# Weights laid out for the DMA, two streams of FFN weights, and a later output projection, in a two-layer transformer kernel

## Chip, cores, metric

One core of one Trainium2 chip. The time is the device time of one execution in microseconds; a kernel is judged by the median of several executions, and compared with another by runs on the same chip. An execution that is profiled also has its own time: the span on a profile's page is about 1.7 us shorter than that time.

## The reference

Two layers, each of them twice layer norm and a residual: a local attention (32 heads of 32, window of 8 positions at distance 2), then a feed-forward part (FFN) with squared ReLU. The sequence has 2048 rows, the model width is 1024, the FFN width 3584; both layers use the same weights.

```python
x = x + A(layernorm(x), wqkv, wo)          # qkv = x @ wqkv; window softmax; @ wo
x = x + B(layernorm(x), w1, b1, w2, b2)    # relu(x @ w1 + b1)**2 @ w2 + b2
x = x + A(layernorm(x), wqkv, wo)
x = x + B(layernorm(x), w1, b1, w2, b2)
```

## The kernel before

The sequence is cut into blocks of 512 rows: 4 per layer, 8 in all, called block 0 to block 7. The program is first recorded as a list of operations with priorities. A planner then orders them for each engine with assumed durations, so that one block's attention on VectorE runs beside another block's matmuls. The FFN matmuls of blocks 1 to 7 use a seven-product scheme: of the seven products of weight quarters, three use raw quarters of w1 ("raw") and four use sums and differences ("made"), which block 0 computes and stores in DRAM.

Weights pass through 1 MB buffers. At most six of them (`w=6`) are live, and they are given out in the order in which they were created. A load is issued when a buffer comes free.

```python
p.caps.update(..., w=6, ..., wl=2)

def weights(self, ap, kt, wide=False):
    b = Buf("8K", "w", [128, 8, 512], BF)
    if wide:   # qkv and wo
        self.dma(lambda: b[:].rearrange("p (a b) n -> p a (b n)", a=4), lambda: ap, (), [(b, 0)], 1.05, name="w")
    ...

def copy_w1(self, after):            # raw quarters of w1, DRAM to DRAM, 21 copies
    for i, (dp, pr) in enumerate(self.order1):
        if pr in (1, 2, 4):
            ...
            self.dma(lambda i=i: self.w1s[i // 4][:, i % 4], lambda k=k, c0=c0: self.w1_v[:, 4 * k:4 * k + 4, c0:c0 + 256], ...)
```

The FFN's first part reads tiles of four products in order of use. The projections take every eighth column of the loaded weights, so that a head's parts land where the attention wants them:

```python
for j, (d, pr) in enumerate(self.order1):          # SF1, blocks 1 to 7
    if j % 4 == 0:
        ...
        self.dma(lambda w=w, n=n: w[:, 0:n], lambda j=j: self.w1s[j // 4][:], ...)
    steps[d](pr, w, j % 4, *rhs[pr])

nc.tensor.matmul(pq[:], wv[:, kd % 4, c0:D:8], xnT[:, :, kd, :], ...)   # SQ, wv a view of [128, 4, 1024]
```

Near the end, the output projection (SW) of block 7 is recorded before the FFN's second part (SF2) of block 6:

```python
if u == NU - 2:
    self.SW(u + 1)
(self.SF2 if u else self.SF2_plain)(u)
```

The softmax here doesn't subtract the row's maximum and nothing guards it: scores larger than these inputs give would overflow.

## Time and profile before

| | before |
|---|---|
| median of the first 4 runs | 1209.71 us (1208.51 to 1210.4) |
| profiled run | 1210.4 us, span 1208.7 us, granted clock 0.997 |
| PE busy | 1182.8 us, 98% |

The first part of the page of the kernel before (busy us, share of the span, number of instructions):

```profile
PE 1182.8 (98%) x6876; PEld 744.2 (62%) x6923; DVE 977.9 (81%) x1551; ACT 670.5 (55%) x1238; POOL 5.0 (0%) x13
```

A busy PE need not be a fast one, so its pitch (the time from the start of one matmul to the start of the next) must be checked: in the timeline below, 40 projections of 512 columns take 8.63 us from start to start (19.79 to 28.42), 215.8 ns each. This is the pitch of every undisturbed run of such matmuls in the trace. Two groups, kept apart by shape, are the projections and their weight loads (count | busy us, mean ns of one | idle before):

```profile
L596 PE MATMUL pq<-xnA,w 128*128 128x512 f16 x1512 | 331.1, 379 | 0.0
L596 PEld LDWEIGHTS <-w 128*128 128x128 bf16 x1512 | 216.6, 143 | 109.4
```

Each matmul lasts 379 ns by the profile, but the next starts 215.8 ns after it, so matmuls overlap. A weight load with the stride of eight columns takes 143 ns. The other 128-column loads take 98 ns, and both fit under 215.8 ns.

What PE waits for, kernel before (us in total, times, longest):

```profile
PE Y L913 <- DMA w<-in_B_w_dram: 5.4, 2, 3.5
PE pk L989 <- POOL grp L240: 5.3, 1, 5.3
PE pq L601 <- DMA w<-in_A_wqkv_dram: 3.7, 2, 2.5
PE Z L859 <- DVE rr L836: 1.7, 4, 0.4
PE Z L913 <- DMA w<-tw: 1.0, 2, 0.6
PE X L913 <- DMA w<-in_B_w_dram: 0.9, 1, 0.9
```

L601 and L596 are the projections, L859 the FFN's first part, L913 its second part. `in_B_w_dram` is w1 or w2, `tw` the made parts of w2. Where these waits lie is seen in PE's timeline of the kernel before (start us, duration, what, [idle before <- releaser]), first in the head:

```profile
12.37 0.66 PE L601 MATMUL pq<-xnA,w 128*128 128x256 f16 x4 [1.21 <-DMA w<-in_A_wqkv_dram]
15.55 1.07 PE L601 MATMUL pq<-xnA,w 128*128 128x256 f16 x4 [2.52 <-DMA w<-in_A_wqkv_dram]
16.41 1.06 PE L532 MATMUL pt<-ident,xn 128*128 128x128 f16 x8
17.27 2.68 PE L601 MATMUL pq<-xnA,w 128*128 128x256 f16 x16
19.79 8.80 PE L596 MATMUL pq<-xnA,w 128*128 128x512 f16 x40
28.42 1.04 PE L601 MATMUL pq<-xnA,w 128*128 128x256 f16 x8
```

and in block 6, where SF1 hands over to SF2:

```profile
1051.20 0.38 PE L370 MATMUL X<-b2r,pick 128*128 128x512 bf16 x1
1052.52 1.67 PE L913 MATMUL X<-w,r 128*128 128x512 bf16 x6 [0.94 <-DMA w<-in_B_w_dram]
...
1057.50 1.04 PE L859 MATMUL Z<-xnB,w 128*128 128x256 f16 x8
1062.02 4.04 PE L913 MATMUL Y<-w,r 128*128 128x512 bf16 x12 [3.48 <-DMA w<-in_B_w_dram]
```

After the wait of 3.48 us, the start-to-start times in the trace are 0.215 us for six matmuls, then 0.427 us: PE runs at half speed for a while. This text calls such matmuls cold. SyncE's own timeline shows why the loads come late: the two loads of wo go first and hold two buffers.

```profile
1039.16 3.83 SPq L305 DMA_DIRECT2D w<-in_A_wo_dram  x2
1046.15 11.91 SPq L305 DMA_DIRECT2D w<-in_B_w_dram  x4
```

### The profile page before, as it was taken

What the parts mean: (1) busy time and instruction counts of PE and PEld (TensorE: products, weight loads), DVE (VectorE), ACT (ScalarE), POOL (GpSimd) and SP (SyncE); (2) the same over time, 40 slices, a digit from 0 to 9 for tenths busy, and PEclk for the clock granted to TensorE, in tenths of its full rate; (3) what the DMA queues carried; (4) which work ended last, traced back from release to release, by engine and by line L of the source; (5) the groups of instructions that cost most, each with busy time, mean ns of one, the idle gap of its engine ahead of it and who ended that gap; (6) DMA issues with size and microseconds to landing.
All of it is one profiled execution on the core that took longest, in us unless ns stands there. A gap on an engine that the chain in (4) does not pass through costs nothing.

```text
span 1208.7 us, 18037 instructions
## 1 busy us (share of the span) xinstructions
PE 1182.8 (98%) x6876; PEld 744.2 (62%) x6923; DVE 977.9 (81%) x1551; ACT 670.5 (55%) x1238; POOL 5.0 (0%) x13
## 2 busy tenths in 40 slices
PE   6999999999999999999999999999999999989998
PEld 4665544557845687456864578555784557834863
DVE  3799999539999499976999589993999949997562
ACT  5546893189702897049940599317981175624640
POOL 1000000000000000000000000000000000000000
PEclk9999999999999999999999999999999999999999
DMA  9679999968999698978999789997899875689964
GB/s 304 201 212 281 299 338 307 316 210 300 267 366 327 215 334 300 353 262 274 347 303 382 251 267 331 332 337 233 296 333 334 296 235 227 222 290 334 324 226 149
DMA packets 209223, 348.03 MB, mean 288 GB/s; under 512 B 67184, under 2 KB 134000, under 8 KB 196336
## 3 DMA queue, kind: packets, MB, share of 16 engines
q1 hardware_dynamic: 197984, 333.22, 82.2%
q10 hardware_dynamic: 7488, 13.63, 3.1%
q0 software_dynamic: 3664, 0.02, 0.4%
q8 instruction: 54, 0.88, 0.3%
q14 instruction: 33, 0.27, 0.1%
HBM read 292.30 MB, written 46.40 MB: 280 GB/s over the span
## 4 chain that ended last, share of the span: by engine, by line
PE 71%; DVE 11%; ACT 10%; DMA 4%; issue 2%; ACTq 1%; SPq 0%; DVEq 0%
PE X L913 14%; PE pq L596 13%; PE X L859 11%; PE Z L913 7%; PE Z L859 6%; DVE P L640 5%; PE py L743 5%; PE py L361 4%; PE ph L774 4%; DVE P L648 3%; PE Y L913 3%; PE Y L859 3%; ACT xn L453 2%; ACT xn L482 2%; ACT xn L478 2%; DMA w<-in_B_w_dram 2%
## 5 line engine op out<-in xcount | busy, mean ns | idle before, releaser
L596 PE MATMUL pq<-xnA,w 128*128 128x512 f16 x1512 | 331.1, 379 | 0.0
L596 PEld LDWEIGHTS <-w 128*128 128x128 bf16 x1512 | 216.6, 143 | 109.4
L859 PEld LDWEIGHTS <-w 128*128 128x128 f16 (+1 forms) x2544 | 248.8, 98 | 39.1 <-issue 3.3
L640 DVE TENSOR_TENSOR P<-q,k 128x2048 f16<-128x2048 f16 x128 | 152.9, 1222 | 85.1 <-ACT q L609 68.5
L913 PEld LDWEIGHTS <-r 128*128 128x128 f16 x1176 | 115.2, 98 | 144.3 <-issue 9.6
L913 PE MATMUL X<-w,r 128*128 128x512 f16 (+1 forms) x777 | 175.9, 379 | 1.4 <-DMA w<-in_B_w_dram 0.9
L609 ACT CAST k<-pq 128x512 f16<-128x512 f32 x64 | 37.6, 587 | 239.5 <-PE pq L596 238.6
L700 DVE TENSOR_TENSOR pr<-pb,v 128x2048 f16<-128x2048 f16 x128 | 154.3, 1220 | 0.2
L859 PE MATMUL X<-T,w 128*128 128x256 f16 x1104 | 135.4, 273 | 0.6 <-ACT u L833 0.6
L648 DVE TENSOR_TENSOR P<-P,P 128x2048 f16<-128x2048 f16 x96 | 116.1, 1216 | 0.1
L743 PE MATMUL py<-w,o 128*128 128x512 bf16 x496 | 111.5, 379 | 0.8
L847 ACT ACTIVATE r<-rr 128x1024 f16<-128x1024 f16 x98 | 102.5, 1062 | 10.8 <-DVE rr L843 9.5
L833 ACT CAST u<-X 128x512 f16<-128x512 f32 x147 | 84.7, 589 | 38.8 <-PE X L859 35.0
L743 PEld LDWEIGHTS <-o 128*128 128x128 bf16 x512 | 50.0, 98 | 59.6
L703 DVE TENSOR_TENSOR pr<-pr 128x1024 f16<-128x1024 f16 x128 | 85.8, 681 | 0.0
L748 DVE TENSOR_TENSOR xm<-py,xt 128x512 f32<-128x512 f32 x64 | 44.0, 690 | 50.1 <-PE py L743 50.0
L836 DVE TENSOR_TENSOR rr<-u,Z 128x512 f16<-128x512 f16 x98 | 65.4, 681 | 18.9 <-ACT u L833 11.0
L478 ACT ACTIVATE xn<-xm 128x1024 f16<-128x1024 f32 x32 | 33.8, 1056 | 59.9 <-DVE xm L748 57.1
L875 ACT ACTIVATE rr<-X,b1T 128x256 f16<-128x256 f32 x98 | 43.2, 482 | 21.6 <-PE X L859 21.4
L706 DVE TENSOR_TENSOR pr<-pr 128x512 f16<-128x512 f16 x128 | 52.1, 415 | 0.1
L913 PE MATMUL Y<-w,r 128*128 128x512 bf16 x191 | 46.2, 388 | 5.9 <-DMA w<-in_B_w_dram 5.4
L843 DVE TENSOR_SCALAR rr<-rr,b1T 128x256 f16<-128x256 f16 (+1 forms) x196 | 50.8, 312 | 0.3
(108 smaller groups left out, 1328.6 us busy)
## 6 DMA issues: line engine op xcount, KB each, us to landing
w<-w1s SPq DMA_DIRECT2D x78, 1024.0 KB, 7.8
w<-tw SPq DMA_DIRECT2D x56, 896.0 KB, 7.7
w<-in_A_wqkv_dram SPq DMA_DIRECT2D x48, 1024.0 KB, 8.5
w<-in_B_w_dram SPq DMA_DIRECT2D x42, 896.0 KB, 7.3
w<-in_A_wo_dram SPq DMA_DIRECT2D x16, 1024.0 KB, 8.4
xt<-xs SPq DMA_DIRECT2D x32, 512.0 KB, 7.4
w<-in_B_w_dram SPq DMA_DIRECT2D x28, 512.0 KB, 7.0
xs<-xo SPq DMA_DIRECT2D x32, 256.0 KB, 7.1
```

The source lines that it names most:

```text
L478: nc.scalar.activation(out=xn[:], in_=xv(), func=ACTF.Identity, accum_out=s1())
L596: nc.tensor.matmul(pq[:], wv[:, kd % 4, c0:D:8], xnT[:, :, kd, :], start=(kd == 0), stop=(kd == KD - 1))
L640: nc.vector.tensor_tensor(cur[:], q[:, c, None, hb * HB:(hb + 1) * HB].to_broadcast([128, W, HB]), _win_ap(k[:, c, :], HALO + hb * HB, HB) ...
L648: nc.vector.tensor_tensor(other[:], other[:], cur[:], ALU.add)
L700: nc.vector.tensor_tensor(pr[:], pb[:], _win_ap(v[:, c, :], HALO + hb * HB, HB), ALU.mult)
L703: nc.vector.tensor_tensor(pr[:, 0:4, :], pr[:, 0:4, :], pr[:, 4:8, :], ALU.add)
L743: nc.tensor.matmul(py[:], o[:, c, tl * 128:(tl + 1) * 128], wos[c // 4][:].rearrange("p (a b) n -> p a (b n)", a=4)[:, c % 4, db * 512:(db ...
L833: p.add("ACT", act(512), lambda: nc.scalar.copy(us[i][:], X[:]), [(X, 0)], [(us[i], 0)], 1.0, name="u")
L836: p.add("DVE", dve(512, False), lambda: nc.vector.tensor_tensor(r[:, :, m, :], us[i][:], bank[:], ALU.add), [(us[i], 0), (bank, 0)], [(r, ...
L847: p.add("ACT", act(1024), lambda: nc.scalar.activation(out=r2[:, f:f + 2, :].rearrange("p a t -> p (a t)"), in_=r[:].rearrange("p a m t -> ...
L859: nc.tensor.matmul(bank[:, a, :], lw[:, k, a * 128:(a + 1) * 128], rhs(k), start=(start and k == 0 and a == 0), stop=(k == 3), skip_group_ ...
L913: nc.tensor.matmul(banks[q][:], left(jj, q), w[:, j, :], start=(start and jj == 0 and b2 is None), stop=(jj == h - 1), skip_group_check=True)
```

## The change

The intent: let every weight load read long contiguous rows, drop the copies inside DRAM, fetch what PE needs first first, and take wo out of the way of w2. The host rearranges the weights; it does no arithmetic on them. Every matmul stays. In core (cut):

```diff
-        self.w1s = [tc.dram_tile([128, min(4, len(self.order1) - i), 4, 256], F16, ...) for i in range(0, len(self.order1), 4)]
+        self.made1 = [o for o in self.order1 if o[1] not in (1, 2, 4)]
+        self.kept1 = [o for o in self.order1 if o[1] in (1, 2, 4)]
+        self.w1s = [tc.dram_tile([128, min(4, len(self.made1) - i), 4, 256], F16, ...) for i in range(0, len(self.made1), 4)]
...                                                  # copy_w1 and its call are removed
-            x, xv = self.load_x(layer, t, after, tag="x0" if u == 0 else "xt")
+            x, xv = self.load_x(layer, t, after, prio=6.5 if u == 1 else None, tag="x0" if u == 0 else "xt")
...
-            ws[nm] = [self.weights(self.wqkv_v[:, 4 * kh:4 * kh + 4, cols[nm]:cols[nm] + D], 8, wide=True) for kh in range(2)]
+            ws[nm] = [self.weights(self.wqkv["qkv".index(nm), kh], 8) for kh in range(2)]
...
-        for j, (d, pr) in enumerate(self.order1):
+        at, ws = [0, 0], [None, None]
+        for d, pr in self.order1:
+            raw = pr in (1, 2, 4)
+            j, at[raw] = at[raw], at[raw] + 1
             if j % 4 == 0:
...
+                src = self.w1r[j // 4, :, 0:n] if raw else self.w1s[j // 4][:]
...
-            steps[d](pr, w, j % 4, *rhs[pr])
+            steps[d](pr, ws[raw], j % 4, *rhs[pr])
...
         mul("B21", *block(1, 0), Y, True)
+        if between:
+            between()
...
             if u == NU - 2:
-                self.SW(u + 1)
-            (self.SF2 if u else self.SF2_plain)(u)
+                seq, self.seq = self.seq, self.seq + 100
+                def between():
+                    back, self.seq = self.seq, seq
+                    self.SW(u + 1)
+                    self.seq = back
+                self.SF2(u, between)
...
+def _layout(inputs):        # on the host
+    wqkv = a.transpose(3, 0, 2, 5, 1, 6, 4).reshape(3, 2, 128, KD, D // 2)
+    ...                     # w1r: tiles of four raw products; w1, w2: rows of 4 KB and 7 KB
```

So there are five parts: (1) rows of 8 KB for wqkv (2 KB before), 4 KB for w1 (512 B) and 7 KB for w2 (1 KB), with unit-stride weight loads of the projections; (2) no copies of w1 in DRAM; (3) k's weights ahead of block 1's x; (4) two streams of w1 tiles, raw and made, in place of one; (5) SW of block 7 is recorded inside SF2 of block 6, so its buffers come after four w2 loads.

## The prediction

> What bounds the kernel now. The page's first part has PE busy 1182.8 of 1208.7 us (98%) at a granted clock of 0.997, nearly all at its steady rate: in PE's timeline, 40 projections of 512 columns follow each other in 8.63 us, 215.8 ns each. The Trainium skill ("TensorE: Matmul & The Clock Gate", Back-to-back issue gap, warm N/2.4 + 2.5 ns) gives 215.8 ns; the trace agrees, so nothing is left inside these runs. The change keeps every matmul: only the 26 us in which PE is idle can be won, under 2.2%.
>
> Improved without gain. The strided weight loads of the projections take 143 ns against 98 ns for contiguous ones (groups of instructions), but both hide under 215.8 ns. The 21 copies of w1 inside DRAM and its 512 B rows (25,088 packets at 255 GB/s while they run; 8 KB 388) load the DMA at 90 to 210 us, where it is full but PE waits 0.4 us. Both: about 0.
>
> Where PE waits (waits of PE, timeline):
> A. Head. Projections start at 12.37 us, the steady stream at 17.27. The weights of k land at 12.33 and 15.50 because 512 KB of x for the next block go ahead; those of q at 18.78 and 21.80, needed at 23.2. The change puts k first and makes rows 8 KB: k lands at about 9.7 and 12.5 (estimate: 2.75 us per MB, not 3.1), projections start at about 11.3, when the transposed tiles are copied, and q, behind the same bytes as before, at about 19.5 to 21.5 becomes the limit. Gain 3.0 us (1.4 if 8 KB rows are no faster; at most 4.2).
> B. Block 1's last FFN part, 331 to 336 us: 2.4 us behind a w2 load issued when a buffer came free at 329.2, landing 6.9 us later. Row size matters little here (a 1 KB-row load alone landed in 5.15 us, a 7 KB-row one in 5.07), but the new split of w1 loads frees buffers in another order: gain about 1.5.
> C. Waits for tw at 624 and 912: 1.3 us, about 0.5 gained.
> D. Block 6, 1051 to 1067 us: two wo loads (issued 1039 and 1043) take buffers ahead of w2, which lands at 1052.5 and 1062.0; PE loses 1.1 and 3.6 us, then runs cold at 427 ns per matmul: 6.6 us in all. The change takes wo after four w2 loads; wo is not needed before about 1078. Gain 6.3.
> E. DVE waits (five of 0.6 us), launch (first matmul at 5.3 us) and tail (3.5 us) stay. New small stalls, above all in the last block, from the two streams of w1: 1 lost.
>
> Sum: 3.0 + 1.5 + 0.5 + 6.3 - 1 = 10.3 us. Predicted 1199 us, 80% range 1194.5 to 1203.5; faster by over 2% 0.01, same 0.98, slower 0.01.
>
> Right if PE busy stays at 1180 to 1184 us and the span falls by idle time alone; weight loads of projections drop to about 98 ns while their matmuls keep their pitch; the steady stream starts at 13 to 15 us with a short wait for q; no wait for w2 and no cold matmuls at 1050 to 1067.
>
> Wrong if matmuls after contiguous weight loads get a shorter pitch; wo comes late and stalls the last attention; the two streams of w1 run out of buffers in every block; or VectorE, over 97% busy from 60 to 210 us, eats the earlier start.

## The result

| | runs | median us | range |
|---|---|---|---|
| before | 16 | 1208.42 | 1203.61 to 1212.49 |
| changed | 11 | 1201.79 | 1200.25 to 1203.42 |

The ratio is 0.9945 with a 95% interval of 0.9931 to 0.9959: 6.6 us less. A ratio is the mean time of one kernel's runs over that of the other's of the same rounds, so it is not quite the ratio of the medians.

The page of the changed kernel, first part:

```profile
PE 1179.9 (98%) x6876; PEld 673.2 (56%) x6923; DVE 979.1 (81%) x1551; ACT 669.7 (56%) x1238; POOL 5.0 (0%) x13
```

Its two groups of the projections:

```profile
L567 PE MATMUL pq<-xnA,w 128*128 128x512 f16 x1512 | 331.2, 379 | 1.4 <-DMA w<-in_A_wqkv_dram 1.4
L567 PEld LDWEIGHTS <-w 128*128 128x128 bf16 x1512 | 147.8, 98 | 178.5 <-DMA w<-in_A_wqkv_dram 2.1
```

The weight loads fell from 143 to 98 ns each and PE's busy time in these matmuls did not move (331.1 and 331.2 us). What PE waits for now:

```profile
PE pk L964 <- POOL grp L240: 5.3, 1, 5.3
PE Z L886 <- DMA w<-tw: 3.3, 2, 1.9
PE Z L832 <- DVE rr L810: 1.6, 4, 0.4
PE pq L567 <- DMA w<-in_A_wqkv_dram: 1.4, 1, 1.4
PE X L886 <- DMA w<-in_B_w_dram: 1.2, 1, 1.2
```

The 5.4 us of the kernel before for w2 are gone; the wait for tw has grown from 1.0 to 3.3 us. PE's timeline of the changed kernel in the head and in block 6:

```profile
11.66 0.60 PE L571 MATMUL pq<-xnA,w 128*128 128x256 f16 x4 [0.42 <-ACT sm L486]
12.80 0.61 PE L571 MATMUL pq<-xnA,w 128*128 128x256 f16 x4 [0.55 <-DMA w<-in_A_wqkv_dram]
...
15.45 2.75 PE L567 MATMUL pq<-xnA,w 128*128 128x512 f16 x12
19.63 6.22 PE L567 MATMUL pq<-xnA,w 128*128 128x512 f16 x28 [1.43 <-DMA w<-in_A_wqkv_dram]
25.68 1.04 PE L571 MATMUL pq<-xnA,w 128*128 128x256 f16 x8
```

```profile
1049.88 0.38 PE L362 MATMUL X<-b2r,pick 128*128 128x512 bf16 x1
1050.09 1.67 PE L886 MATMUL X<-w,r 128*128 128x512 bf16 x6
...
1055.08 1.04 PE L832 MATMUL Z<-xnB,w 128*128 128x256 f16 x8
1055.95 6.21 PE L886 MATMUL Y<-w,r 128*128 128x512 bf16 x27
```

The same eight matmuls (L601, now L571) start at 25.68 instead of 28.42 us: the head is 2.74 us shorter. In block 6 the waits and the cold matmuls are gone.

The clock in the head is a second difference. In the table of windows (start:end, length, busy us and counts of PE, PEld, DVE, ACT and POOL, then the granted clock, DMA share, GB/s), the kernel before shows PE at half clock for 3.4 us after its wait of 2.52 us:

```profile
15.40:18.80 3.40, 3.25 (x20) 2.77 (x21) 0.69 (x1) 1.50 (x2) 0.00 (x0) 0.50 1.21 346
```

The changed kernel was granted 1.00 there. With the stretch in block 6 (1063.3 to 1066.7 us), the kernel before ran 6.8 us at half clock, which costs about 3.4 us (an estimate: half of 6.8), almost half of what the change won between these two profiles. Its timed runs fit: 42 of them, in the experiments below, were granted 0.996 to 0.999, those at 0.996 took 1210.1 us in the mean and those at 0.999 1206.1 us; the changed kernel's were granted 0.999 to 1.000.

Where the rest went needs a finer count. I took, from each trace, the start-to-start times of consecutive matmuls, subtracted the pitch (215.8 ns for 512 columns, in proportion for fewer), added up what was left over 0.05 us, and left out gaps of one unrecorded matmul (0.19 to 0.235 us without a releaser, outside the head and block 6). This "PE loss" starts at the first matmul, 5.3 us. In the row of block 6 about 0.6 us of either figure is such gaps.

| PE loss, us, from:to us | before | changed | difference | predicted |
|---|---|---|---|---|
| head, 0:60 | 7.7 | 5.0 | -2.7 | -3.0 (A) |
| 60:300 | 1.3 | 1.6 | +0.3 | 0 |
| block 1's SF2, 300:345 | 2.4 | 0.0 | -2.4 | -1.5 (B) |
| blocks 1 to 6, 345:1030 | 4.4 | 8.2 | +3.8 | -0.5 (C) |
| block 6, SF1 to SF2, 1030:1080 | 7.1 | 0.6 | -6.5 | -6.3 (D) |
| block 7, 1080:end | 0.0 | 0.5 | +0.5 | +1 (E, anywhere) |
| sum | 22.9 | 15.9 | -7.0 | -10.3 |

The sum agrees with the spans of the two pages (1208.7 and 1201.7). Between 60 and 300 us, where the copies were taken out, the loss did not fall, although the DMA share at 90 to 120 us fell from 1.00 to 0.48 in the table of windows.

The loss of 3.8 us in the middle is three waits: for the first tw load of block 3 at 620 us (1.6 us; 0.5 before), for w2 in block 4 at 755 us (1.3; none before), and for the first tw load of block 5 at 911 us (2.1; 0.8 before).

### The profile page after: what moved, and what is told of

Same layout as the page of the kernel before. It is cut to its first block, busy times and chain, and to the rows that moved or that the text cites. A ratio compares the mean times of both kernels' runs of the same rounds, so it can differ in the third digit from the quotient of the medians.

```text
span 1201.7 us, 18027 instructions
## 1 busy us (share of the span) xinstructions
PE 1179.9 (98%) x6876; PEld 673.2 (56%) x6923; DVE 979.1 (81%) x1551; ACT 669.7 (56%) x1238; POOL 5.0 (0%) x13
## 4 chain that ended last, share of the span: by engine, by line
PE 67%; DVE 14%; ACT 12%; DMA 3%; issue 2%; ACTq 1%; SPq 0%; DVEq 0%
PE X L886 14%; PE pq L567 12%; PE X L832 11%; PE Z L886 7%; DVE P L610 6%; PE Z L832 6%; PE py L353 4%; DVE P L618 4%; PE Y L886 3%; PE py L713 3%; ACT xn L423 3%; ACT xn L452 3%; PE ph L744 3%; PE Y L832 3%; ACT xn L448 3%
## 5 line engine op out<-in xcount | busy, mean ns | idle before, releaser
L567 PE MATMUL pq<-xnA,w 128*128 128x512 f16 x1512 | 331.2, 379 | 1.4 <-DMA w<-in_A_wqkv_dram 1.4
L832 PEld LDWEIGHTS <-w 128*128 128x128 f16 (+1 forms) x2648 | 259.0, 98 | 41.6 <-issue 3.6
L567 PEld LDWEIGHTS <-w 128*128 128x128 bf16 x1512 | 147.8, 98 | 178.5 <-DMA w<-in_A_wqkv_dram 2.1
L832 PE MATMUL X<-T,w 128*128 128x256 f16 x1160 | 142.3, 273 | 0.8 <-ACT u L807 0.8
L832 PE MATMUL Z<-xnB,w 128*128 128x256 f16 x392 | 49.3, 272 | 1.6 <-DVE rr L810 1.6
```

Of the source, the lines that this page charges most:

```text
L567: nc.tensor.matmul(pq[:], wv(w, c0, kd), xnT[:, :, kd, :], start=(kd == 0), stop=(kd == KD - 1))
L832: nc.tensor.matmul(bank[:, a, :], w[:, wi, k, a * 128:(a + 1) * 128], rhs(k), start=(start and k == 0 and a == 0), stop=(k == 3), skip_gro ...
```

## The experiments

Theories at the start. A: the wo loads held two buffers ahead of w2 in block 6; moving SW gives that part. B: two w1 streams keep two part-used tiles alive, so buffers come free later, the w2 loads are issued later and the tw load after them comes late; this takes 3 to 4 us back. H: in the head the order of loads brings the start forward, and 8 KB rows bring q forward. Rivals: R1, the 7 KB rows of w2 ended the waits of block 6; R2, the 7 KB rows of w2, not the streams, cause the new waits.

### 1. Only the place of SW (`sw_only`, `sw_only_again`)

The kernel before with this alone:

```diff
+        if between:
+            between()            # after B21 in SF2
-            if u == NU - 2:
-                self.SW(u + 1)   # and SF2(u, between) as in the change
```

> The kernel before, with only the place of the last output projection changed (its two wo loads after the first four w2 loads of block 6). Theory A (the wo loads held two buffers ahead of w2): the two waits for w2 at 1051 to 1062 us and the cold matmuls after them go, the rest of the trace stays; minus 6.4 us, ratio 0.9947. Rival R1 (the 7 KB rows of w2, which this kernel does not have, ended those waits): a wait of over 2 us for w2 stays in block 6, ratio 0.998 to 1.000.

Measured: 1203.95 us against 1208.0, ratio 0.9973 (0.9952 to 0.9993). Two of six runs lay at 1208 and 1208.8, so it was run again:

> The kernel before with only the place of the last output projection changed, once more, because two of its six runs lay 4 us above the others and its interval is wide. Theory A: 6.8 us gone in block 6, about 2 us of new waits for w1 in the last block, so ratio 0.9960 to 0.9970 as the four low runs and the new waits say; 0.9947 if the new waits were chance.

Measured: 1203.91 us against 1208.0, ratio 0.9973 (0.9951 to 0.9996), again with one run at 1209. In both profiles the waits for w2 in block 6 and the cold matmuls are gone, without long rows of w2. In exchange block 7 waits for w1 (1.6 and 1.1 us). From PE's waits in `sw_only`:

```profile
PE Y L859 <- DMA w<-w1s: 1.5, 1, 1.5
```

So A holds as a mechanism and R1 falls, but the time won is 3.3 us by the ratio or 4.1 us by the medians, not the 6.4 us that I expected. Part of the difference is the new wait. The other part can be the sample: the two profiled runs of the kernel before took 1210.4 and 1211.3 us, near the slow end of its 1203.6 to 1212.5 us. The clock tells the rest: the three high runs of the twelve were granted 0.995 or 0.996, the nine low ones 0.998 to 1.000. So the high runs had more cold matmuls; none of them was profiled, so where is not known.

### 2. Everything but the place of SW (`sw_back`)

```diff
             if u == NU - 2:
-                self.SF2(u, between)
+                self.SW(u + 1)
+            (self.SF2 if u else self.SF2_plain)(u)
```

> The changed kernel with the last output projection put back before block 6's second FFN part; all layouts and both w1 streams stay. Theory A: PE waits for w2 again at about 1045 to 1060 us, some 6 us with the cold matmuls; ratio 0.999 to 1.001. Rival R1 (row size): no such wait, ratio as the whole change, 0.9945.

Measured: 1205.44 us against 1208.0, ratio 0.9974 (0.9954 to 0.9993). PE waits for w2 in block 6 again, in spite of the 7 KB rows:

```profile
PE Z L886 <- DMA w<-tw: 3.8, 2, 2.0
PE Y L886 <- DMA w<-in_B_w_dram: 2.1, 1, 2.1
PE X L886 <- DMA w<-in_B_w_dram: 1.4, 1, 1.4
```

The loss in block 6 is 3.8 us here, not some 6: the longer wait was 2.1 us, and no cold matmuls followed (0.216 us from start to start). A wait of this size can do it, though: in block 5 of the same execution, after a wait of 1.98 us for tw, the matmuls came 0.427 us apart for 3.4 us.

```profile
910.12 2.96 PE L886 MATMUL Z<-w,s 128*128 128x512 f16 x7 [1.98 <-DMA w<-tw]
```

The rest of the change is then worth about as much (0.9974) as the place of SW alone (0.9973).

### 3. One stream of w1 in the changed kernel (`one_stream`)

Tiles of four products in order of use as before; the raw part of a tile comes from the arranged input and the made part from DRAM, in two transfers.

```diff
+                raw, made = self.parts1[j // 4]
+                slot = {o: i for i, o in enumerate(raw + made)}
+                self.dma(lambda ...: w[:, 0:nr].bitcast(BF), lambda ...: self.w1r[j // 4, :, 0:nr], ...)
+                self.dma(lambda ...: w[:, nr:nr + nm], lambda ...: self.w1s[j // 4][:], ...)
-            steps[d](pr, ws[raw], j % 4, *rhs[pr])
+            steps[d](pr, w, slot[d, pr], *rhs[pr])
```

> The changed kernel with the w1 tiles of before: four products in order of use to a tile, its raw part loaded from the arranged input, its made part from DRAM scratch, in two transfers to the same buffer; no copies inside DRAM. Theory B (two streams keep two part-used tiles alive, so the buffers of the next w2 loads come free later): the waits at about 620 and 911 us for tw fall from 1.6 and 2.1 us to about 0.5 and 0.8, the 1.3 us for w2 at 755 goes; the wait of 2.4 us in block 1 may come back; ratio 0.9920 without it, 0.9940 with it. Rival R2 (those waits come from the 7 KB rows of w2): they stay, ratio 0.9945.

Measured: 1201.02 us against 1208.0, ratio 0.9939 (0.9923 to 0.9955). The waits went as B says: none at 620 and 755 us, 0.6 us at 908. In PE's waits between 340 and 1030 us of this version, one line is left for tw:

```profile
PE Z L889 <- DMA w<-tw: 0.5, 1, 0.5
```

The loss from 345 to 1030 us is 3.7 us. SyncE's timeline of block 3 shows what differs. In the changed kernel, then with one stream:

```profile
602.20 7.89 SPq L304 DMA_DIRECT2D w<-in_B_w_dram  x4
614.09 5.10 SPq L304 DMA_DIRECT2D w<-tw  x4
```

```profile
597.64 0.33 SPq L303 DMA_DIRECT2D w<-in_B_w_dram  x1
...
603.04 6.27 SPq L303 DMA_DIRECT2D w<-in_B_w_dram  x3
615.05 5.09 SPq L303 DMA_DIRECT2D w<-tw  x4
```

With one stream the first w2 load is issued 17.4 us ahead of the first tw load, with two streams 11.9 us. With two the last w2 load landed at 616.04, 1.95 us after the tw load was issued; with one it landed at 615.40, 0.35 us after. PE needs tw about 4.6 us after its issue in both. But 1.0 us came back in block 1 and 1.6 us in block 7, so little of it could be won, and the time does not show it.

### 4. Short rows of w2 in the changed kernel (`w2_rows1k`)

```diff
-        return self.weights(self.w2[k2, n2, :, half * h:(half + 1) * h, :], h)
+        w2 = self.w2.rearrange("(k j p) (m n) -> k m p j n", k=2, p=128, m=2)
+        return self.weights(w2[k2, n2, :, half * h:(half + 1) * h, :], h)
```

> The changed kernel with w2 in its old layout, so rows of 1 KB instead of 7 KB; the same instructions in the same order otherwise. Theory B: the waits at 620, 755 and 911 us stay within 0.5 us each and block 6 has no wait for w2; ratio 0.9935 to 0.9950. Rival R2: the waits in blocks 3 to 5 shrink by 3 us in all, ratio 0.992. Rival R1: a wait of over 2 us for w2 comes back in block 6, ratio 0.997 or more.

Measured: 1201.38 us against 1208.0, ratio 0.9943 (0.9925 to 0.9961). Here B alone missed: with two streams and short rows the two tw waits are gone too. Between 340 and 1030 us only this is left for the DMA (at 615 and 759 us):

```profile
PE Y L890 <- DMA w<-in_B_w_dram: 1.0, 2, 0.6
```

The loss from 345 to 1030 us is 4.3 us, against 8.2 in the changed kernel. No wait for w2 came back in block 6, so R1 falls a second time. For R2 the waits went, but the time did not follow (expected 0.992). Here the first w2 load was issued 12.8 us ahead of the first tw load, little more than the 11.9 us of the changed kernel, so the late issue that B names does not make the wait by itself.

### 5. Both kernels once more (`before_again`, `after_again`)

> The kernel before once more, unchanged, as a control: ratio 1.000 within 0.0015. In its profile the two waits for w2 in block 6 come again; the question is their size. If the cold matmuls after the second wait are a matter of chance, the loss there lies between 3.5 us (without) and 7 us (with them).

> The changed kernel once more, unchanged, for a second profile and a time beside the others of this call. Ratio 0.9945 within 0.0015. Theory B: the waits for tw near 620 and 911 us (1.6 and 2.1 us) are there again, as they were in the version with the last output projection put back; if they are chance, they differ by more than 1 us.

Measured: `before_again` 1208.72 against 1208.41 us, ratio 1.0001 (0.9986 to 1.0015). The loss in block 6 is 8.6 us (about 8.0 without the gaps of unrecorded matmuls), over the 7 us that I expected at most. `after_again` 1200.6 us, ratio 0.9933 (0.9919 to 0.9947). The tw waits are there again (1.9 and 2.2 us), so they are not chance; the w2 wait at 755 us is not, so that one is. One of the two tw waits was put down by the profile to a VectorE operation ("DVE r"); the tw load landed at 620.17 us, 0.04 us before the matmul started, so it was the DMA.

### 6. The head in parts (`k_first`, `x_first`)

`k_first` is the kernel before with the new order of loads; `x_first` the changed kernel with the old order:

```diff
# k_first: + prio=6.5 if u == 1 else None      x_first: - the same
```

> The kernel before, with only the order of the first loads changed: the weights of k ahead of the x of block 1; rows stay 2 KB. Theory H (the order brings the start forward, the rows of 8 KB bring q forward): k lands about 1.6 us earlier than 12.33 and 15.50, q where it did (18.8 and 21.8), so PE starts earlier and then waits for q: gain 0.6 to 1.4 us, ratio 0.9990. Rival (order alone gives the whole 2.7 us): ratio 0.9978 and q lands before 20.5.

> The changed kernel with the x of block 1 again ahead of the weights of k; rows stay 8 KB. Theory H: k lands at about 11.7 and 14.3 us, q at 17 and 19.6 as in the changed kernel; PE gets q just when it has done k; it loses at most 1 us against the changed kernel, ratio 0.9945 to 0.9955. Rival (the order gives the gain): it loses 2 us or more, ratio 0.9962 or more.

Measured: `k_first` 1206.86 us, ratio 0.9989 (0.9977 to 1.0001); `x_first` 1201.09 us, ratio 0.9938 (0.9926 to 0.9950). The start of the same eight matmuls says more:

| | k lands, us | q lands, us | eight matmuls start |
|---|---|---|---|
| before | 12.33, 15.50 | 18.78, 21.80 | 28.42 |
| k_first | 10.79, 13.96 | 18.69, 21.77 | 26.19 |
| x_first | 12.51, 15.08 | 17.66, 20.24 | 28.07 |
| changed | 10.15, 12.76 | 16.98, 19.58 | 25.68 |

In these pairs the order gives 2.2 to 2.4 us, more than the 0.6 to 1.4 of H, and long rows 0.35 to 0.5 us. But the pairs differ in the clock too. `before` and `x_first` ran at half clock for 3.4 us in the head (`x_first` from 16.4 us), about 1.7 us each by the estimate above; `k_first` and the changed kernel did not. `sw_only` has the head of the kernel before and stayed at full clock:

```profile
15.32 0.66 PE L601 MATMUL pq<-xnA,w 128*128 128x256 f16 x4 [2.37 <-DMA w<-in_A_wqkv_dram]
26.65 1.04 PE L601 MATMUL pq<-xnA,w 128*128 128x256 f16 x8
```

So at full clock the order gives 0.46 us (26.65 to 26.19) and the long rows 0.51 us (26.19 to 25.68); the rest of the 2.74 us is the cold stretch. Of five profiles with x first, four went cold in the head; of nine with k first, none. The order seems to keep PE warm by cutting the wait for k's second half from 2.0 to 2.6 us down to 1.5 us or less, but with this few profiles that is likely, not shown. H, which counted waits alone, was near for the order's own share (0.46 us against 0.6 to 1.4) and did not see the clock.

The landings of q show that the rows are faster (1 MB per 2.6 us instead of 3.0 to 3.1), but little of it was won: the planner's order changed as well, `k_first` ran 20 of the 40 projections ahead of the second half of q and waited 0.63 us, the changed kernel ran 12 and waited 1.43 us. My 1.4 us rested on q being needed at 23.2 us. Only its first half is: the second half is needed four matmuls (0.86 us) later. The times of `x_first` and the changed kernel (0.9938 and 0.9933) do not resolve the difference of 2.4 us in the head. Three of the five runs of `x_first` were granted 1.000, which a stretch of 3.4 us at half clock would have brought to 0.999, so most of them had none; that profile of `x_first` also lost only 5.2 us from 345 to 1030 us.

### 7. More of k before q (`after_k5`, `one_k5`)

```diff
-        order = [("k", c0) for c0 in range(3)]
+        order = [("k", c0) for c0 in range(5)]        # and c0 - 5 for q in the loop
```

> The changed kernel with five groups of k instead of three ahead of the first group of q. Theory H (q, behind the same bytes, is what the head waits for): the wait of 1.4 us for q at 19.6 us goes, the head is 1.4 us shorter; waits in blocks 3 to 5 as in the changed kernel; ratio 0.9925 to 0.9935. Rival (VectorE, which then gets its first q later, gives it back by block 1): same time as the changed kernel.

> The same order of k and q with the w1 tiles of before (one stream, each tile loaded in a raw and a made part). No wait for q in the head, waits for tw and w2 in blocks 2 to 5 of at most 1 us in all; about 1 us faster than the changed kernel with this order: ratio 0.9920. If the two streams cost nothing that shows in the time, the two versions are equal within 0.5 us.

Measured: `after_k5` 1200.05 us, ratio 0.9935 (0.9912 to 0.9958); `one_k5` 1198.97 us, ratio 0.9929 (0.9909 to 0.9950), both against 1208.0. The wait for q is gone in both profiles, and the eight matmuls start at 24.45 and 24.29 us. The head's loss is 3.7 us. VectorE does not give it back: the loss from 60 to 300 us is 1.6 and 1.7. The two versions differ by 1.1 us in the medians, within their intervals. The predicted ratio of 0.9920 for `one_k5` was missed, though inside the interval.

### 8. Two streams, short w2 rows, more of k first (`k5_rows1k`)

The edits of 4 and 7 together.

> The changed kernel with five groups of k first and with w2 in rows of 1 KB: a second profile of two w1 streams with short w2 rows. If row size matters beside the streams (the one profile so far had 4.3 us of PE loss between 345 and 1030 us, the profiles with 7 KB rows 5.2 to 8.2), the loss there is again under 5 us and the two waits for tw at 620 and 908 us stay away; if that profile was chance, the loss is 5 us or more and a tw wait of over 1 us is back. Head as in the version with five groups of k first. Ratio 0.9915 to 0.9935.

Measured: 1198.72 us against 1208.55, ratio 0.9917 (0.9903 to 0.9930), the lowest time. The loss from 345 to 1030 us is 3.7 us and the tw waits stay away:

```profile
PE Z L836 <- DVE rr L814: 1.6, 4, 0.4
...
PE Z L890 <- DMA w<-in_B_w_dram: 0.5, 1, 0.5
```

It beats both kernels in the median. Its interval lies wholly below the changed kernel's first one (0.9931 to 0.9959) and overlaps the second (0.9919 to 0.9947), so against the changed kernel it is likely, not proved, to be faster.

### What the profiles of all versions say about tw

Time from issue to landing of the first tw load of SF2:

| w1 streams, w2 rows | version | block 3, us | block 5, us |
|---|---|---|---|
| two, 7 KB | changed | 6.12 | 6.75 |
| | after_again | 6.44 | 6.96 |
| | sw_back | 6.89 | 6.89 |
| | x_first | 4.55 | 6.97 |
| | after_k5 | 6.52 | 4.60 |
| two, 1 KB | w2_rows1k | 5.26 | 4.65 |
| | k5_rows1k | 4.79 | 4.85 |
| one, 7 KB | one_stream | 4.70 | 5.37 |
| | one_k5 | 4.92 | 4.73 |
| one, 1 KB | before | 5.07 | 5.32 |
| | before_again | 4.64 | 4.96 |
| | k_first | 4.73 | 4.56 |
| | sw_only | 4.91 | 4.70 |
| | sw_only_again | 4.74 | 4.58 |

With both new features, 8 of 10 landings take 6.1 to 7.0 us; with one of them or none, 18 of 18 take 4.5 to 5.4 us. PE needs the data about 4.6 us after the issue, so the slow ones cost about 2 us each. Blocks 2 and 4, where PE did not wait for that load, agree: 7 of 10 over 5.7 us with both features, 18 of 18 under 5.5 us without. The two features do it together, and undoing either undoes it. Why long w2 rows still in flight delay the next load, and short ones do not (in `w2_rows1k` w2 was in flight for 3.1 us after the issue, and tw still took 5.26 us), was not tested and stays open.

## Why the prediction was right or wrong

The time fell inside the predicted range (1194.5 to 1203.5) and the class, within 2%, was right. The predicted gain was 10.3 us; it was 6.6 us by the times and 7.0 us by the profiles.

- What bounds it: right. PE's pitch at full clock stayed at 215.8 ns with either weight load, and the span moved with PE's idle and cold time alone. PE busy was to stay at 1180 to 1184 us and is 1179.9.
- Strided weight loads and DRAM copies worth nothing: shown for the loads (143 to 98 ns, busy 331.1 and 331.2 us). For the copies, the loss at 60 to 300 us did not fall with the DMA load there; leaving them out alone was not run. The Trainium skill ("SBUF — State Buffer", Door 1: The DMA port swizzle) says that SBUF has 16-byte lines and that each access crossing to a new line pays; the old loads step 16 bytes per column and took 143 ns, the new ones 98 ns, so the trace agrees.
- A, the head: 2.74 us against 3.0, in part by luck. The k landings were within 0.5 us of the predicted ones and q became the limit, as foretold. But q landed at 16.98 and 19.58 us, not at 19.5 to 21.5, PE asked for it earlier too, and about 1.7 of the 2.74 us is a cold stretch of the kernel before that A does not name (experiment 6).
- B, block 1: 2.4 us against 1.5. The 1.5 was given without a sum behind it. The loss is 0.0 in all seven profiles with two streams, with either row length; it is 1.0 and 1.4 us in the two with one stream and the other parts of the change, and 0.8 to 2.7 us in the five of the kernel before and its variants. So the two streams end it. That they do so by the order in which buffers come free was argued and not traced.
- C and E, the term that failed: "about 0.5 gained" on tw, and 1 us lost elsewhere, "above all in the last block". In its place the tw waits grew by 2.3 us, a w2 wait of 1.3 us came once, and the loss from 345 to 1030 us rose by 3.8 us (by 3.5 in the second pair of profiles, 3.3 to 6.8). The text listed this ("the two streams of w1 run out of buffers") among what could go wrong and did not cost it. The last block lost only 0.5 us.
- D, block 6: right in mechanism (experiments 1 and 2) and right in the profile (6.5 us against 6.3), oversized in time: 3.3 to 4.1 us alone, 3.8 us of loss when undone. The 6.6 us were read from one execution, and under 2 us of them are cold matmuls (6.6 less the waits of 1.1 and 3.6 us). The Trainium skill ("TensorE: Matmul & The Clock Gate", What's actually happening) says PE drops to half its clock after an idle window of about 3.4 us, and that the window is free-running, so the point varies. The traces agree on the half clock (0.427 against 0.216 us), on stretches of 3.4 us and on the varying point: after waits of about 3.5 us in block 6, matmuls started 0.427 us apart, after six warm ones in one execution and at once in another. They do not agree that a whole window must be idle. In `sw_back` the clock fell at 910.3 us although PE had been busy for 1.4 of the 3.4 us before. Waits of 1.95 to 2.55 us were followed by cold matmuls in five places (four heads and block 5 of `sw_back`), others of that size were not, such as 2.37 us in the head of `sw_only` and 2.08 us in block 6 of `sw_back`.

## What to carry to other kernels

Where one engine runs at its pitch for 98% of the time, list its waits one by one and ask of each which buffer or byte ends it; in this kernel a shorter weight load and a lighter DMA elsewhere won nothing. When a stream is split in two, cost the part-used tile that each stream holds: here the loads behind it were issued later, and together with another harmless change (long rows) that brought a wait that neither brought alone. A wait that turns PE cold costs more than its own length, and not in every execution. So read the granted clock of each stage and of each timed run before taking the difference of two profiles for the gain, or sharing it out between the parts of a change.

## What the Trainium skill lacked or had wrong

- "TensorE: Matmul & The Clock Gate", Back-to-back issue gap, gives a sustained rate of about 131 ns for a 512-column matmul in a stream of weight loads and matmuls, and gives N/2.4 + 2.5 ns, which the prediction used, only for an isolated matmul, as an over-count in a stream. Here 40 such pairs in a row took 215.8 ns each, at the formula.
- "Perfetto Trace Analysis", Identifying the Most-Contended Engine, has PE's headroom judged by MFU (the share of peak FLOP/s reached) and by the busy share of weight loads. The second misleads here: it fell from 62% to 56% (744.2 to 673.2 us) while the projections' busy time stayed at 331 us: it measured the stride of the loads, not headroom.
- "TensorE: Matmul & The Clock Gate", LDWEIGHTS, has the time of a weight load depend on the column count alone. Here 128 columns took 98 ns at unit stride and 143 ns at a step of eight bf16 columns; the line rule of "SBUF — State Buffer" is not linked there.
- "DMA: Bandwidth & Descriptors" has nothing on what long rows still in flight do to the landing of the next load. Here, with two streams, 7 KB rows went with 6.1 to 7.0 us to landing for the next load in 8 of 10 cases, and 1 KB rows with 4.65 to 5.26 us in 4 of 4.
- "TensorE: Matmul & The Clock Gate", What's actually happening, puts PE in the half-rate state after at least one idle window of about 3.4 us. Here it fell to half clock after waits of 1.95 to 2.55 us in five places, once with PE busy for 1.4 of the 3.4 us before.
